# Top-k attention with a squared-ReLU MLP on one core: top-k on folded halves, a mask applied in PSUM, and a planned order

## The chip, the cores and the metric

One core of a Trainium2 chip runs the whole program. The metric is the device time of one execution in microseconds (us). Three runs of the kernel before gave 2025.48, 2029.64 and 2031.14 us; their median is 2029.64 us. The engines are named as in the profile: PE is the matrix engine (PEld its weight loads), DVE the vector engine, ACT the scalar engine, POOL the GpSimd engine, SP the engine that issues the DMAs.

## The reference

```python
def _attn_ref(q, k, v):                       # each (8, 8, 576, 64) float32
    scores = scale * np.matmul(q, k.transpose(0, 1, 3, 2))     # scale = 1/8
    kth = np.partition(scores, -32, axis=-1)[..., -32:-31]
    scores = np.where(scores >= kth, scores, -1000000000.0)
    attn = np.exp(scores - np.max(scores, axis=-1, keepdims=True))
    attn = attn / (np.sum(attn, axis=-1, keepdims=True) + 1e-09)
    return np.matmul(attn, v)

def _moe_ref(x, w_in, w_out):                 # x (4608, 512), w_in (512, 2048), w_out (2048, 512)
    r = np.maximum(x @ w_in, 0.0)
    return (r * r) @ w_out
```

The attention output of all heads is laid out as 4608 tokens by 512 and goes through the second function. So each of 8 x 8 x 576 = 36864 query rows has to find the 32nd largest of its 576 scores.

## The kernel before, in words

**Tiling.** Two heads make a pair, 32 pairs in all. The 1152 query rows of a pair are cut into 9 blocks of 128 rows (block 4 has 64 rows of either head), so there are 288 blocks. All of a block lives on 128 partitions, with its 576 scores along the free dimension.

**One block.** PE transposes q and k of the pair once (L238 to L265) and computes the scores in float32, with 64 rows of contraction (L316, L317). ACT copies them from PSUM to `Ssb` (L328). DVE finds the 32nd largest of 576 values in four rounds: MAX8 gives the eight largest, MATCH_REPLACE8 takes them out (L341 to L347; each MATCH_REPLACE8 brings a short MATCH_VALUE_LOAD), and a compare writes a bias `Bsb`, 0 or -30000 (L348). POOL adds bias and scores (L362). ACT takes the exponential with its row sum (L380), DVE the reciprocal (L390), ACT scales an identity matrix by it (L402), PE multiplies by that matrix, which transposes and normalises at once (L417, L418), ACT copies the result to bfloat16 `pT` (L430, L431). When the 9 blocks of a pair are there, PE computes the product with v, with 64 output rows per head (L461, L468), and ACT puts it into `xT`.

Every DVE and every ACT instruction waits for the one before it on its engine (`_run`, L117 to L128), since each round reads what the last one wrote.

**MLP.** Tokens go through it in 9 chunks of 512: 16 groups of 4 matmuls into one PSUM bank `Hps` (L546), ReLU and square on ACT (L563, L565), then 16 matmuls for each 128 tokens (L580) into the same bank, a copy (L600) and a DMA out.

**What sets the order.** Every step is a task with a hand-written time, counted in blocks (L434 to L443 for the attention, L492 to L498 for the product with v, L638 to L647 for the MLP); each engine runs its tasks sorted by that time and waits on semaphores. SP issues four weight loads first, each waiting for POOL's cast of the one before (L179 to L185), and only then the loads of q, k and v.

```python
            run_dve(lambda: vec.max(m8[:, 0, :], ssb[:, :]))
            run_dve(lambda: vec.match_replace(T1[:, :], m8[:, 0, :], ssb[:, :], NEG_MR))
            run_dve(lambda: vec.max(m8[:, 1, :], T1[:, :]))
```

Of the kernel before, what the change touches and what calls it, by code (L numbers as in the profile page):

```python
# [3 lines left out]
ALU = mybir.AluOpType  # L5
ACTF = mybir.ActivationFunctionType
FP32 = mybir.dt.float32
BF16 = mybir.dt.bfloat16

NEGB = -30000.0  # L10
NEG_MR = -3.0e38
TOPK = 32
P = 128


def bass_top_k_attn__then__act_relu_squared_kernel(
# [7 lines left out]
    n_batches_override=None,  # L24
):
    Bq, Hq, S, Dh = q.shape
    assert Hq == 8 and S == 576 and Dh == 64, (Bq, Hq, S, Dh)
    NB = Bq if n_batches_override is None else n_batches_override
# [15 lines left out]
    ident_bf = sb("ident_bf", [P, P], BF16)

    Rq = [sb(f"Rq{i}", [P, 5, 2, Dh]) for i in range(2)]
    Rk = [sb(f"Rk{i}", [P, 5, 2, Dh]) for i in range(2)]
    Rv = [sb(f"Rv{i}", [P, 5, 2, Dh]) for i in range(2)]
    qT = [sb(f"qT{i}", [P, S]) for i in range(2)]
    kT = [sb(f"kT{i}", [P, S]) for i in range(2)]  # L50
    vbf = [sb(f"vbf{i}", [P, 5, 2, Dh], BF16) for i in range(2)]

    KSB, KM, KE, KD, KZ = 5, 2, 3, 3, 4
    Ssb = [sb(f"Ssb{i}", [P, S]) for i in range(KSB)]
    T1 = sb("T1", [P, S])
    T2 = sb("T2", [P, S])
    Bsb = [sb(f"Bsb{i}", [P, S]) for i in range(2)]
    Smask = [sb(f"Smask{i}", [P, S]) for i in range(KM)]
    negm = [sb(f"negm{i}", [P, 1]) for i in range(KM)]
    M8 = [sb(f"M8_{i}", [P, 4, 8]) for i in range(2)]  # L60
    Ebf = [sb(f"E{i}", [P, S], BF16) for i in range(KE)]
    Zt = sb("Z", [P, KZ])
    rZt = sb("rZ", [P, KZ])
    Dt = [sb(f"Dt{i}", [P, P], BF16) for i in range(KD)]
    pT = [sb(f"pT{i}", [P, 5, 2 * S], BF16) for i in range(2)]
    xT = sb("xT", [P, NCT, NTOK], BF16)

# [48 lines left out]

    def _run(engkey, eng, op, inc):  # L117
        s, n = prog[engkey]
        if n > 0:
            eng.wait_ge(s, n)  # L120
        ins = op()
        if inc is None:
            ins.then_inc(s, 1)
        else:
            ins.then_inc(inc[0], inc[1])
            eng.nop().then_inc(s, 1)
        prog[engkey][1] = n + 1
        return ins  # L128

    def run_dve(op, inc=None):  # L130
        return _run("dve", nc.vector, op, inc)

    def run_act(op, inc=None):
        return _run("act", nc.scalar, op, inc)

    def block_parts(g):
        if g < 4:
            return [(0, 128 * g, 128, 0)]
        if g == 4:
            return [(0, 512, 64, 0), (1, 0, 64, 64)]  # L140
        qs = 128 * g - 576
        return [(1, qs, 128, 0)]

    def gp_setup():
        g = nc.gpsimd
        g.memset(ident32[:], 0.0).then_inc(s_set, 1)
        g.wait_ge(s_set, 1)
        g.affine_select(ident32[:], ident32[:], [[-1, P]], ALU.not_equal, 1.0,
                        base=0, channel_multiplier=1).then_inc(s_set, 1)
        g.wait_ge(s_set, 2)  # L150
        g.tensor_copy(ident_bf[:], ident32[:]).then_inc(s_set, 1)

    task("gp", -100, 0, gp_setup)

    WST4 = wst[:, :].rearrange("p (ct f) -> p ct f", ct=NCT)
    WST8 = wst[:, :].rearrange("p (fb o) -> p fb o", fb=8)

    def gp_weights():
        g = nc.gpsimd
        g.wait_ge(s_dw, 16 * 1)  # L160
        g.wait_ge(s_set, 3)
        g.tensor_copy(win[:, :, 0:1024], WST4).then_inc(s_wc, 1)
        g.wait_ge(s_dw, 16 * 2)
        g.wait_ge(s_wc, 1)
        g.tensor_copy(win[:, :, 1024:2048], WST4).then_inc(s_wc, 1)
        g.wait_ge(s_dw, 16 * 3)
        g.wait_ge(s_wc, 2)
        g.tensor_copy(wo[:, 0:8, :], WST8).then_inc(s_wc, 1)
        g.wait_ge(s_dw, 16 * 4)
        g.wait_ge(s_wc, 3)  # L170
        g.tensor_copy(wo[:, 8:16, :], WST8).then_inc(s_wc, 1)

    task("gp", -50, 0, gp_weights)

    def sp_weights():
        spe = nc.sync
        wi = moe_w_in.rearrange("(ct p) f -> p ct f", p=P)
        wo_ap = moe_w_out.rearrange("(fb p) o -> p fb o", p=P)
        spe.dma_start(WST4, wi[:, :, 0:1024]).then_inc(s_dw, 16)  # L179
        spe.wait_ge(s_wc, 1)  # L180
        spe.dma_start(WST4, wi[:, :, 1024:2048]).then_inc(s_dw, 16)
        spe.wait_ge(s_wc, 2)
        spe.dma_start(WST8, wo_ap[:, 0:8, :]).then_inc(s_dw, 16)
        spe.wait_ge(s_wc, 3)
        spe.dma_start(WST8, wo_ap[:, 8:16, :]).then_inc(s_dw, 16)  # L185

    task("sp", -90, 0, sp_weights)

    def dq_val(pi):
        return 128 * (pi // 2 + 1)  # L190

    def dv_val(pi):
        return 64 * (pi // 2 + 1)

    def sp_pair_dma(pi):
        def fn():
            spe = nc.sync
            b, hp = pi // NHP, pi % NHP
            slot = pi % 2
            if pi >= 2:  # L200
                spe.wait_ge(s_qkt, 4 * (pi - 1))
                spe.wait_ge(s_cv, pi - 1)
                spe.wait_ge(s_dq[slot], dq_val(pi - 2))
                spe.wait_ge(s_dvr[slot], dv_val(pi - 2))
            for (src, R, semx) in ((q, Rq[slot], s_dq[slot]),
                                   (k, Rk[slot], s_dq[slot]),
                                   (v, Rv[slot], s_dvr[slot])):
                for h in range(2):
                    sh = src[b, 2 * hp + h, :, :]
                    spe.dma_start(  # L210
                        R[:, 0:4, h, :],
                        sh[0:512, :].rearrange("(tb p) d -> p tb d", p=P),
                    ).then_inc(semx, 16)
                    spe.dma_start(
                        R[0:64, 4, h, :],
                        sh[512:576, :],
                    ).then_inc(semx, 16)
        return fn

    for pi in range(NPAIR):  # L220
        task("sp", 9 * pi - 18, 0, sp_pair_dma(pi))

    def pe_qk_transpose_round(pi, r):
        def fn():
            pe = nc.tensor
            slot = pi % 2
            base = 4 * pi
            if r == 0:
                pe.wait_ge(s_set, 2)
                pe.wait_ge(s_dq[slot], dq_val(pi))  # L230
                for (sx, vx) in ops_waits[("tq", pi)]:
                    pe.wait_ge(sx, vx)
            else:
                pe.wait_ge(s_qke, base + r)
            mm = None
            if r == 0:
                for tb in range(4):
                    mm = pe.matmul(  # L238
# [473 lines left out]
```

## Time and profile before

| | |
|---|---|
| median of three runs | 2029.64 us (2025.48 to 2031.14) |
| profiled execution, first to last instruction | 2029.7 us |
| DVE busy | 1730.8 us, 85% |
| PE busy | 1383.1 us, 68% |
| ACT busy | 1076.7 us, 53% |
| POOL busy | 419.6 us, 21% |
| granted PE clock, mean | 0.667 of full speed |

The profile's page gives only the span of the profiled execution, and that equals the median of the runs, so nothing measurable lies around it. A busy PE is not a PE at its peak, since its matmuls overlap; the granted clock has two levels, 0.5 (1.2 GHz) and 1.0 (2.4 GHz), and a value between them is a mean over a stretch.

### The profile page before, as it was taken

Reading aid. Unit: us, or ns where it says so; the run is one execution under the profiler, and the core shown is the slowest. Engines: PE = TensorE matmul, PEld = TensorE weight load, DVE = VectorE, ACT = ScalarE, POOL = GpSimd, SP = SyncE. Lnnn points to the kernel's source line nnn. Section 1 sums busy time; section 2 is a strip of 40 time slices with the busy share of each in tenths; the row PEclk is TensorE's granted clock in tenths of the full one; section 3 lists DMA queues with packets and bytes.
Section 4 is the critical chain, followed back from the end, with each engine's and each line's share of the span. In section 5 each row is a group of like instructions: output and inputs, shape, how many; then the busy total and the mean of one; then the engine's idle time right before and its main releaser. Section 6 shows DMA issues by size and latency. Waiting matters only on the chain.

```text
span 2029.7 us, 23123 instructions
## 1 busy us (share of the span) xinstructions
PE 1383.1 (68%) x4764; PEld 632.4 (31%) x4832; DVE 1730.8 (85%) x3456; ACT 1076.7 (53%) x2597; POOL 419.6 (21%) x299
## 2 busy tenths in 40 slices
PE   0556567777667776877667767777678776778576
PEld 0223333333333332333333333333333333333222
DVE  0899999998999999998999989999999989998500
ACT  0354555664566554664566555664566645664434
POOL 3122222222222222221222222221222222222100
PEclk9995555776566755677567765677555865666569
DMA  5100000001000100001000110001000100000000
GB/s 188 30 18 18 18 18 18 18 9 31 18 18 18 34 23 18 1 23 34 18 18 18 29 28 1 18 19 39 18 18 18 28 12 18 18 1 21 0 16 26
DMA packets 125197, 47.65 MB, mean 23 GB/s; under 512 B 117376, under 2 KB 117376, under 8 KB 125056
## 3 DMA queue, kind: packets, MB, share of 16 engines
q1 hardware_dynamic: 125056, 46.16, 8.6%
q8 instruction: 40, 0.66, 0.1%
q14 instruction: 101, 0.83, 0.1%
HBM read 36.70 MB, written 9.44 MB: 23 GB/s over the span
## 4 chain that ended last, share of the span: by engine, by line
DVE 55%; PE 20%; issue 12%; ACT 8%; DMA 1%; DVEq 1%; POOL 1%; ACTq 0%; SPq 0%; POOLq 0%
DVE T L342 8%; DVE T L346 8%; DVE T L344 8%; DVE M L345 8%; DVE M L347 8%; DVE M L343 8%; PE Hps L546 7%; DVE M L341 7%; PE Hps L580 5%; PE Ops L461 3%; ACT gT L563 2%; PE Tst L417 2%; DVE rZ L390 1%; ACT pT L430 1%; PE Ops L253 1%
## 5 line engine op out<-in xcount | busy, mean ns | idle before, releaser
L362 POOL TENSOR_TENSOR Smask<-Ssb,Bsb 128x576 f32<-128x576 f32 x288 | 404.2, 1403 | 1453.1 <-DVE Bsb L348 1448.0
L316 PE MATMUL Sps<-kT,qT 64*128 64x512 f32 (+1 forms) x640 | 499.2, 957 | 0.3 <-ACT kT L283 0.3
L417 PE MATMUL Tst<-Dt,E 128*128 128x128 bf16 x1152 | 151.7, 276 | 447.3 <-ACT pT L431 443.4
L341 DVE MAX8 M<-Ssb 128x8 f32<-128x576 f32 x288 | 214.5, 745 | 104.6 <-ACT Ssb L328 55.4
L402 ACT ACTIVATE Dt<-ident_bf,rZ 128x128 bf16<-128x128 bf16 x288 | 116.1, 403 | 306.0 <-DVE rZ L390 305.2
L546 PE MATMUL Hps<-xT,win 128*128 128x512 bf16 x531 | 221.8, 552 | 29.9 <-ACT gT L563 20.7
L417 PEld LDWEIGHTS Tst<-Dt,E 128*128 128x128 bf16 x1152 | 90.2, 117 | 486.1 <-ACT E L380 468.1
L317 PEld LDWEIGHTS Sps<-kT,qT 64*128 64x128 f32 (+1 forms) x640 | 156.3, 262 | 247.9 <-issue 247.9
L380 ACT ACTIVATE E<-Smask,negm 128x576 bf16<-128x576 f32 x288 | 223.1, 775 | 9.4
L345 DVE MAX8 M<-T 128x8 f32<-128x576 f32 x288 | 219.1, 761 | 9.8
L347 DVE MAX8 M<-T 128x8 f32<-128x576 f32 x288 | 219.1, 761 | 9.8
L343 DVE MAX8 M<-T 128x8 f32<-128x576 f32 x288 | 219.0, 760 | 9.8
L342 DVE MATCH_REPLACE8 T<-M,Ssb 128x576 f32<-128x576 f32 x288 | 213.8, 742 | 0.0
L346 DVE MATCH_REPLACE8 T<-M,T 128x576 f32<-128x576 f32 x288 | 213.8, 742 | 0.0
L344 DVE MATCH_REPLACE8 T<-M,T 128x576 f32<-128x576 f32 x288 | 213.7, 742 | 0.0
L328 ACT COPY Ssb<-Sps 128x576 f32<-128x576 f32 x288 | 184.2, 639 | 9.5 <-PE Sps L317 7.0
L580 PE MATMUL Hps<-wo,gT 128*128 128x512 bf16 x553 | 169.3, 455 | 11.8 <-ACT osb L600 4.6
L563 ACT ACTIVATE gT<-Hps 128x512 bf16<-128x512 f32 x144 | 85.7, 595 | 156.8 <-PE Hps L546 120.0
L430 ACT CAST pT<-Tst 128x512 bf16<-128x512 f32 x288 | 162.7, 565 | 2.3 <-PE T L418 2.3
L348 DVE TENSOR_SCALAR Bsb<-Ssb,M 128x576 f32<-128x576 f32 x288 | 149.8, 520 | 10.3
L316 PEld LDWEIGHTS Sps<-kT,qT 64*128 64x128 f32 (+1 forms) x640 | 120.4, 254 | 110.8 <-issue 102.5
L461 PE MATMUL Ops<-pT,vbf 128*64 128x512 bf16 (+1 forms) x320 | 135.8, 559 | 4.7 <-issue 3.3
(45 smaller groups left out, 1156.0 us busy)
## 6 DMA issues: line engine op xcount, KB each, us to landing
out_dram<-osb SPq DMA_DIRECT2D x36, 256.0 KB, 2.0
Rq<-in_q_dram SPq DMA_DIRECT2D x64, 128.0 KB, 2.3
Rk<-in_k_dram SPq DMA_DIRECT2D x64, 128.0 KB, 2.4
Rv<-in_v_dram SPq DMA_DIRECT2D x64, 128.0 KB, 2.4
wst<-in_moe_w_in_dram SPq DMA_DIRECT2D x2, 2048.0 KB, 7.9
wst<-in_moe_w_out_dram SPq DMA_DIRECT2D x2, 2048.0 KB, 8.9
Rq<-in_q_dram SPq DMA_DIRECT2D x64, 16.0 KB, 2.1
Rk<-in_k_dram SPq DMA_DIRECT2D x64, 16.0 KB, 2.1
```

The source lines that it names most:

```text
L316: last = pe.matmul(sps[rb:rb + nr, 0:512], qTi, kTi[:, 0:512])
L341: run_dve(lambda: vec.max(m8[:, 0, :], ssb[:, :]))
L342: run_dve(lambda: vec.match_replace(T1[:, :], m8[:, 0, :], ssb[:, :], NEG_MR))
L343: run_dve(lambda: vec.max(m8[:, 1, :], T1[:, :]))
L344: run_dve(lambda: vec.match_replace(T2[:, :], m8[:, 1, :], T1[:, :], NEG_MR))
L345: run_dve(lambda: vec.max(m8[:, 2, :], T2[:, :]))
L346: run_dve(lambda: vec.match_replace(T1[:, :], m8[:, 2, :], T2[:, :], NEG_MR))
L347: run_dve(lambda: vec.max(m8[:, 3, :], T1[:, :]))
L362: g.tensor_tensor(sm[:, :], ssb[:, :], bsb[:, :], ALU.add).then_inc(s_gm, 1)
L417: last = pe.matmul(Tst[:, j, :], e[:, 128 * j:128 * j + 128], d[:, :])
L546: last = pe.matmul(Hps[:, 0:ln], win[:, ct, fb * 128:fb * 128 + 128], xT[:, ct, ts:ts + ln], start=(ct == 0), stop=(ct == NCT - 1),)
L580: last = pe.matmul(Hps[0:nr, 0:DMODEL], gT[:, fb, o:o + nr], wo[:, fb, :], start=(fb == 0), stop=(fb == NFB - 1),)
```

## The change

The kernel is written anew around the same data types. For each query block:

- The 576 scores are kept as two halves of 288. DVE takes the larger of each column pair (`m`). POOL gets the smaller of each pair exactly, by adding the two bit patterns as integers (`t1`) and subtracting that of the larger (`lo`). DVE runs the four MAX8 and three MATCH_REPLACE8 on the 288 larger values and one MAX8 on the 288 smaller ones. The 32nd largest of all is then the largest of: the 32nd of the larger ones, and for j = 1 to 8 the smaller of the j-th of the smaller ones and the (32-j)-th of the larger ones (`mn`, `kt`). It holds if fewer than 8 of the smaller ones are among the 32 largest; a flag at the end says whether a row broke that, and if so the whole program is run a second time with 16 smaller ones.
- POOL makes a mask tile `w` in bfloat16 with two instructions of 576 columns: it is 2 to the 60th where a score falls short, and else the row's largest score, but not under zero.
- PE computes the scores a second time, transposed (keys on partitions), and subtracts the mask in the same PSUM bank by a matmul with the negative identity. ACT takes the exponential straight into the layout that the product with v needs.
- The product with v is token-major: 65 columns per head and block, the last one of ones, so that the row sum comes with it. DVE takes its reciprocal and multiplies; PE transposes the result back.
- Blocks go in groups of 2, 2, 2 and 3 (one block of either head side by side), and the DVE instructions of a group alternate between its blocks. The two heads' float32 matmuls are issued alternately, one on partitions 0 to 63 and one on 64 to 127, into different banks.
- The MLP runs per batch (576 tokens) with two PSUM banks per group; of the last batch the square is on DVE. Weights come in 16 loads of 512 KB, behind the first loads of q and k.
- A planner (`Plan.schedule`) runs all steps through an event loop with an estimated duration each, on every engine the ready step with the lowest priority value first, and hands out the buffers. The engines get the resulting fixed orders; `Emitter` puts waits only where a step needs something not yet known to be done, on its own engine too.

```diff
-            run_dve(lambda: vec.max(m8[:, 0, :], ssb[:, :]))
...
-            run_dve(lambda: vec.tensor_scalar(bsb[:, :], ssb[:, :], m8[:, 3, 7:8], NEGB,
-                                              ALU.is_lt, ALU.mult), inc=(s_tk, 1))
...
-            g.tensor_tensor(sm[:, :], ssb[:, :], bsb[:, :], ALU.add).then_inc(s_gm, 1)
...
+    GROUPS = [[(0, 0), (1, 0)], [(0, 1), (1, 1)], [(0, 2), (1, 2)], [(0, 3), (1, 3), (2, 4)]]
+    PER = 3.6
...
+                            for half in range(2):
+                                ks = HALF * half
+                                for h in range(2):
+                                    ins = mm(bank(tiles[h], half)[:, 0:HALF],
+                                             x[64 * h:64 * h + 64, 0, 128 * gi:128 * gi + 128],
+                                             x[64 * h:64 * h + 64, 1, ks:ks + HALF], True)
...
+                    for i in range(nb):
+                        pl.op("gp", .85, tg - 1 + .8 * i, lambda t=t1[i], s=st[i]: gp.tensor_tensor(
+                            at(t)[:, :].bitcast(I32), at(s)[:, 0:HALF].bitcast(I32),
+                            at(s)[:, HALF:S].bitcast(I32), ALU.add), r=[st[i]], w=[t1[i]], take=[t1[i]])
+                        dve(.38, lambda t=m[i], s=st[i]: vec.tensor_tensor(
+                            at(t)[:, :], at(s)[:, 0:HALF], at(s)[:, HALF:S], ALU.max),
...
+                        pl.op("gp", .85, tg + .8 + .8 * i, lambda t=t1[i], m_=m[i], l=lo[i]: gp.tensor_tensor(
+                            at(l)[:, :].bitcast(I32), at(t)[:, :].bitcast(I32),
+                            at(m_)[:, :].bitcast(I32), ALU.subtract), r=[t1[i], m[i]], w=[lo[i]], take=[lo[i]])
+                    for rnd in range(4):
+                        for i in range(nb):
+                            src = m[i] if rnd == 0 else wk[i]
+                            last[i] = dve(.38, lambda s=src, i=i, rnd=rnd, A=A: vec.max(
+                                A(i, 8 * rnd, 8 * rnd + 8), at(s)[:, :]), r=[src], w=[a])
...
+                            f = (lambda s=src, d=wk[i], i=i, rnd=rnd, A=A: vec.match_replace(
+                                at(d)[:, :], A(i, 8 * rnd, 8 * rnd + 8), at(s)[:, :], NEG))
...
+                        bl[i] = dve(.38, lambda l=lo[i], i=i, B=B: vec.max(B(i, 0), at(l)[:, :]),
...
+                    mn = dve(.1, lambda a=a, bt=bt, nb=nb, n0=n0, nr=nr: vec.tensor_tensor(
...
+                    sh = dve(.08, lambda a=a, nb=nb, n0=n0: vec.tensor_scalar(
...
+                    kt = dve(.1, lambda a=a, nb=nb, n0=n0, nr=nr: vec.tensor_reduce(
...
+                        pl.op("gp", .65, tw + 1.3 * i, lambda y=y, s=st[i], n=n0 + i: gp.tensor_scalar(
+                            at(y)[:, :], at(s)[:, :], nkth[:, n:n + 1], STEEP, ALU.add, ALU.mult),
...
+                        pl.op("gp", .65, tw + 1.3 * i + .65, lambda y=y, w=w, n=n0 + i: gp.tensor_scalar(
+                            at(w)[:, :], at(y)[:, :], BIG, shift[:, n:n + 1], ALU.min, ALU.max),
...
+                        for j in range(2):
+                            ins = mm(o[:, 128 * j:128 * j + 128], at(ws[(h, j)])[:, kc:kc + nk],
+                                     neg_bf[:, :], False)
...
+                                for h in range(2):
+                                    qkT(bank(e, h)[:, 0:nq], qk, h, 128 * kb, 128, q0, nq, True)
+                                for h in range(2):
+                                    ins = masked(bank(e, h)[:, 0:nq], h, 128 * kb, 128, ws, wz)
...
+                                mm(o[:, 65 * u:65 * u + 65], pp[:, kb, h, 128 * j:128 * j + 128],
+                                   vv[:, 4 * h + kb, :], first_)
...
+                    pl.op("dve", .15, tt + 9, lambda av=av, rz=rz, nu=nu: vec.reciprocal(
...
+                    pl.op("dve", .45, tt + 9.1, lambda av=av, rz=rz, xr=xr, nu=nu: vec.tensor_tensor(
...
+            val = eng.value_load(flag[0:1, 0:1], min_val=0, max_val=P)
+            with eng.If(val > 0):
+                em.emit(again, e, eng)
```

## Rows read from the trace of the kernel before

**Rows 1.** The page's first part: busy time and share of the span by engine.
```profile
PE 1383.1 (68%) x4764; PEld 632.4 (31%) x4832; DVE 1730.8 (85%) x3456; ACT 1076.7 (53%) x2597; POOL 419.6 (21%) x299
```
**Rows 2.** Waits: engine, line, whom it waited for: us in total, times, longest.
```profile
DVE M L341 <- ACT Ssb L328: 55.4, 1, 55.4
...
PE Ops L238 <- DMA Rk<-in_k_dram: 47.4, 1, 47.4
...
DVE M L341 <- issue: 44.5, 28, 3.5
```
**Rows 3.** Timeline of DVE, one block in mid-run: start us, us, line, operation.
```profile
1007.11 0.52 DVE L348 TENSOR_SCALAR Bsb<-Ssb,M 128x576 f32<-128x576 f32 x1
1007.55 0.16 DVE L390 RECIPROCAL rZ<-Z 128x1 f32<-128x1 f32 x1
1007.62 0.74 DVE L341 MAX8 M<-Ssb 128x8 f32<-128x576 f32 x1
1008.40 0.09 DVE L342 MATCH_VALUE_LOAD T<-M,Ssb 128x8 f32 x1
1008.48 0.74 DVE L342 MATCH_REPLACE8 T<-M,Ssb 128x576 f32<-128x576 f32 x1
...
1013.35 0.52 DVE L348 TENSOR_SCALAR Bsb<-Ssb,M 128x576 f32<-128x576 f32 x1
```
**Rows 4.** Busy time by engine over the top-k stage.
```profile
55.00:1905.00 1850.00, 1292.76 (x4465) 601.40 (x4525) 1730.62 (x3455) 1023.46 (x2505) 402.92 (x288) 0.65 0.08 19
```
**Rows 5.** Groups of POOL by shape: busy us, mean ns; then one instruction in its timeline.
```profile
L362 POOL TENSOR_TENSOR Smask<-Ssb,Bsb 128x576 f32<-128x576 f32 x288 | 404.2, 1403 | 1453.1 <-DVE Bsb L348 1448.0 <-ACT Ssb L328 5.1
L162 POOL CAST win<-wst 128x4096 bf16<-128x4096 f32 x1 | 3.6, 3602 | 6.9 <-DMA wst<-in_moe_w_in_dram 6.9
L151 POOL CAST ident_bf<-ident 128x128 bf16<-128x128 f32 x1 | 0.3, 291 | 0.1
...
1007.71 1.41 POOL L362 TENSOR_TENSOR Smask<-Ssb,Bsb 128x576 f32<-128x576 f32 x1 [4.84 <-DVE Bsb L348]
```
**Rows 6.** Timeline of PE at clock 1.0: a whole block, small matmuls, block 4.
```profile
144.82 1.12 PE L316 MATMUL Sps<-kT,qT 64*128 64x512 f32 x2
145.79 0.33 PE L317 MATMUL Sps<-kT,qT 64*128 64x64 f32 x2
147.43 0.38 PE L417 MATMUL Tst<-Dt,E 128*128 128x128 bf16 x4 [1.31 <-ACT pT L431]
147.74 0.24 PE L418 MATMUL T<-Dt,E 128*64 128x128 bf16 x1
...
452.22 0.60 PE L238 MATMUL Ops<-ident,Rq 128*128 128x128 f32 x4
...
472.15 1.08 PE L316 MATMUL Sps<-kT,qT 64*64 64x512 f32 x4
473.06 0.29 PE L317 MATMUL Sps<-kT,qT 64*64 64x64 f32 x4
```
**Rows 7.** Timeline of PE in the MLP at the end, at 1.0.
```profile
1981.47 1.02 PE L546 MATMUL Hps<-xT,win 128*128 128x512 bf16 x4 [0.72 <-issue]
...
2014.13 3.61 PE L580 MATMUL Hps<-wo,gT 128*128 128x512 bf16 x16 [0.77 <-ACT osb L600]
```
**Rows 8.** Two-microsecond stretches of the MLP at the end; granted clock third from the end.
```profile
1964.00:1966.00 2.00, 2.00 (x6) 0.72 (x5) 0.00 (x0) 0.00 (x0) 0.00 (x0) 0.50 0.00 0
1966.00:1968.00 2.00, 1.60 (x7) 0.48 (x5) 0.00 (x0) 0.36 (x1) 0.00 (x0) 0.90 0.00 0
...
1988.00:1990.00 2.00, 1.04 (x4) 0.31 (x4) 0.00 (x0) 1.50 (x3) 0.00 (x0) 1.00 0.00 0
```
**Rows 9.** SP's timeline at the start: one of a pair's 12 issues.
```profile
45.33 0.59 SPq L210 DMA_DIRECT2D Rv<-in_v_dram  x1
```
**Rows 10.** ACT's exponential and copy by shape: busy us, mean ns.
```profile
L380 ACT ACTIVATE E<-Smask,negm 128x576 bf16<-128x576 f32 x288 | 223.1, 775 | 9.4
L328 ACT COPY Ssb<-Sps 128x576 f32<-128x576 f32 x288 | 184.2, 639 | 9.5 <-PE Sps L317 7.0 <-issue 1.9 <-DVE Bsb L348 0.2
```

More of the change, by code (lines that the diff above doesn't have):

```diff
@@ L2 @@
+import heapq
 import concourse.bass as bass
@@ L6, with __init__, take, find @@
 ACTF = mybir.ActivationFunctionType
+AX = mybir.AxisListType
 FP32 = mybir.dt.float32
 BF16 = mybir.dt.bfloat16
-NEGB = -30000.0
-NEG_MR = -3.0e38
+I32 = mybir.dt.int32
+P = 128
 TOPK = 32
-P = 128
+NEG = -3.0e38
+BIG = 2.0 ** 60
+STEEP = -(2.0 ** 90)
+class Pool:
+    def __init__(self, name, n):
+        self.name, self.n = name, n
+        self.free = list(range(n))
+        self.last = [None] * n
+        self.made = self.taken = 0
+    def take(self, tl):
+        if self.name != "psum" and tl.num != self.taken:
+            return None
+        s = self.find(tl.width)
+        if s is not None:
+            self.taken += 1
+        return s
+    def find(self, width):
+        if width == 1:
+            if not self.free:
+                return None
+            if self.name == "psum":
+                half = [s for s in self.free if (s ^ 1) not in self.free]
+                s = half[0] if half else self.free[0]
+            else:
+                s = self.free[0]
+            self.free.remove(s)
+            return s
+        for s in self.free:
+            if s % width == 0 and all(s + i in self.free for i in range(width)):
+                for i in range(width):
+                    self.free.remove(s + i)
+                return s
+        return None
+    def undo(self, s, width):
+        self.taken -= 1
+        self.give(s, width)
+    def give(self, s, width):
+        self.free.extend(range(s, s + width))
@@ new lines, with __init__ @@
+class Tile:
+    def __init__(self, pool, width=1):
+        self.pool, self.width = pool, width
+        self.slot = None
+        self.num = pool.made
+        pool.made += 1
+        self.ops = []
+        self.writers = []
+        self.left = 0
+        self.prev = []
+        self.taker = None
+class Op:
+    __slots__ = ("eng", "dur", "prio", "fn", "deps", "tiles", "takes", "n", "users", "start", "end",
+                 "idx", "sem", "val", "ndma", "seq", "vc", "waits", "wars", "later")
@@ L23, in bass_top_k_attn__then__act_relu_squared_kernel @@
     out: bass.AP,
[L24 removed]
 ):
[L26 to L28 removed]
+    NB, H, S, D = q.shape
+    assert H == 8 and S == 576 and D == 64, (NB, H, S, D)
+    HALF = S // 2
     NHP = 4
@@ L649, in bass_top_k_attn__then__act_relu_squared_kernel @@
-    n_tot = NMOUT
-    n_even = (n_tot + 1) // 2
-    n_odd = n_tot // 2
-    def sp_final():
-        spe = nc.sync
-        spe.wait_ge(s_dout[0], 16 * n_even)
-        spe.wait_ge(s_dout[1], 16 * n_odd)
-    task("sp", chunk_t0(NCHUNK - 1) + 200, 0, sp_final)
-    with nc.Block() as blk:
-        def emit(eng):
-            for _, _, _, fn in sorted(tasks[eng], key=lambda x: (x[0], x[1], x[2])):
-                fn()
+        for i in range(16):
+            s = tile("ws")
+            if i < 8:
+                ct, half = divmod(i, 2)
+                src = wi[:, ct, 1024 * half:1024 * half + 1024]
+                dst = win[:, ct, 1024 * half:1024 * half + 1024]
+                view = lambda s: at(s)[:, :]
+            else:
+                fb = 2 * (i - 8)
+                src = wo_ap[:, fb:fb + 2, :]
+                dst = wo[:, fb:fb + 2, :]
+                view = lambda s: at(s)[:, :].rearrange("p (f o) -> p f o", f=2)
+            pl.op("sp", 4.0, 20 + 4 * i, lambda s=s, src=src, view=view: [nc.sync.dma_start(view(s), src)],
+                  w=[s], take=[s], ndma=1, sem=lambda o: f"ws{o.takes[0].slot}")
+            weights.append(pl.op("gp", 1.1, 40 + 6 * i, lambda s=s, dst=dst, view=view: gp.tensor_copy(dst, view(s)),
+                                 r=[s]))
@@ new lines, in setup, with fin @@
+        setup.pre = [i1, i2, i3] + ones + [f1]
+        return weights
+    main = build(False, True, setup)
+    for o in main.ops:
+        if o not in setup.pre and o.eng == "pe":
+            o.deps.update(setup.pre)
+    def fin(pl, waits):
+        vec, pe = nc.vector, nc.tensor
+        t = Tile(psum)
+        c = pl.op("dve", .35, 1e6, lambda: vec.tensor_tensor(
+            fcmp[:, :], b8all[:, :, 7], nkth[:, :], ALU.add), after=waits)
+        d = pl.op("dve", .35, 1e6, lambda: vec.tensor_reduce(fone[:, 0:1], fcmp[:, :], AX.X, ALU.max), after=[c])
+        f = pl.op("dve", .1, 1e6, lambda: vec.tensor_scalar(
+            fone[:, 0:1], fone[:, 0:1], 0.0, None, ALU.is_gt), after=[d])
+        g = pl.op("pe", .1, 1e6, lambda: pe.matmul(bank(t)[0:1, 0:1], fone[:, 0:1], fone[:, 1:2],
+                                                   start=True, stop=True), w=[t], take=[t], after=[f])
+        return pl.op("dve", .1, 1e6, lambda: vec.tensor_copy(flag[:, :], bank(t)[0:1, 0:1]), r=[t])
@@ new lines, in bass_top_k_attn__then__act_relu_squared_kernel @@
+    flagged = fin(main, list(kths))
+    span = main.schedule()
+    em.number(main)
+    again = build(True, False, None)
+    t_end = max(o.end for o in main.ops) + 1
+    again.schedule(t_end)
+    em.number(again)
+    out_waits = [(em.dma[k][0], 0, k) for k in em.dma if k.startswith("o")]
+    first_tot = {}
+    for pl_, store in ((main, first_tot),):
+        for o in pl_.order["sp"]:
+            if o.idx[0][1].startswith("o"):
+                store[o.idx[0]] = o.idx[1]
+    second_tot = {}
@@ new lines, in bass_top_k_attn__then__act_relu_squared_kernel, with emit @@
+    for o in again.order["sp"]:
+        if o.idx[0][1].startswith("o"):
+            second_tot[o.idx[0]] = o.idx[1]
+    with nc.Block() as blk:
+        def emit(e, eng):
+            em.emit(main, e, eng)
+            if e == "sp":
+                for kk, vv in first_tot.items():
+                    eng.wait_ge(em.sem(kk), vv)
+            if e != "dve" or True:
+                eng.wait_ge(em.sems["dve"], flagged.idx[1])
+            val = eng.value_load(flag[0:1, 0:1], min_val=0, max_val=P)
+            with eng.If(val > 0):
+                em.emit(again, e, eng)
+                if e == "sp":
+                    for kk, vv in second_tot.items():
+                        eng.wait_ge(em.sem(kk), vv)
```

1113 lines of the change are left out of this document (552 added, 561 removed).

## The prediction

> **What bounds the kernel now.** I read the engine shares first [rows 1]: DVE is busy for 85% of the span, nobody else for more than 68%. The waits say whether it rests inside its stage [rows 2]: it waits once for 55.4 us, for the first scores, and after that 44.5 us in 28 places, all of them with no releaser. The stage view gives 1850 us from first to last DVE work, 1730.62 of them busy [rows 4]. The timeline of one block shows why [rows 3]: from one TENSOR_SCALAR to the next are 6.24 us, and 288 x 6.24 = 1797 us; the stage is 1850 / 1797 = 1.029 of that. Then comes a tail without DVE, 2029.7 - 1905 = 125 us, in which the MLP catches up. So the time is 55 (start) + 1850 (top-k on DVE) + 125 (MLP): those three terms are what the change must move. The span equals the median of the runs, so I sum against 2029.7.
>
> **DVE, the new top-k.** One price per column: MAX8 over 576 columns takes 0.74 us and a one-column RECIPROCAL 0.16 [rows 3], so a column costs (0.74 - 0.16) / 575 = 1.0 ns and an instruction over 288 columns 0.16 + 0.29 = 0.45 us; the same for MATCH_REPLACE8, which took 0.74 too. How far apart do they start? An instruction that depends on its forerunner comes 0.04 us after its end (MAX8 lasts 0.74, the next starts 0.78 after it). One that does not starts early: RECIPROCAL begins 0.44 us after a TENSOR_SCALAR of 0.52, and MAX8 0.07 us after RECIPROCAL [rows 3]. The new order alternates between the blocks of a group, so most forerunners belong to another block: 0.45 - 0.08 = 0.37 us per instruction, and 0.08 more for each MATCH_VALUE_LOAD. Per block:
> - five MAX8 (four on the larger values, one on the smaller): 5 x 0.37 = 1.85
> - three MATCH_REPLACE8 with their loads: 3 x 0.45 = 1.35
> - one maximum of the halves, a two-input operation that before never ran on DVE: between 0.37 (as MAX8) and 0.49 (it waits for ACT's copy just ahead); I take 0.49.
>
> That is 3.69 us, times 288 = 1063 us. Small instructions per pair: three for each of four groups (`mn`, `sh`, `kt`), between 0.07 and 0.20 us by the RECIPROCAL row, and as they follow one another in part I take 0.13, 12 x 0.13 = 1.56; and twice a reciprocal (0.20) with a multiply of up to 320 columns (0.16 + 0.32 + 0.04 = 0.52), 1.44. Together 3.0 x 32 = 96 us. The sum 1159 us times the 1.029 that this stage loses today gives 1193 us, 37.3 us per pair. With every doubt settled low it is 1028 + 57 = 1085; with every instruction held until its forerunner ends it is 9 x 0.49 plus 3 x 0.08 = 4.65 per block, (1339 + 123) x 1.029 = 1504.
>
> **POOL** gets most of the new work. Its old 128x576 add took 1.403 us; casts of 4096 and 128 columns took 3.602 and 0.291, so 0.83 ns a column over 0.18 us [rows 5]. Integer add and subtract over 288 columns: 0.18 + (1.403 - 0.18) / 2 = 0.79 each. Mask in two one-input instructions of 576 columns: 0.18 + 0.48 = 0.66 each, if they run like a cast; like the two-input add, 1.40. With 0.1 us between instructions (an estimate from the spacing of the chain's dependent steps on DVE, 0.04, and doubled for POOL) a block costs 2 x 0.79 + 2 x 0.66 + 0.4 = 3.3 us; the casts of v add 1.1 per pair: 30.8 us per pair, under DVE's 37.3. MAX8 at 1007.62 and MATCH_REPLACE8 at 1008.48 ran beside POOL's add of 1007.71 [rows 3, 5] and took no longer than elsewhere, so I charge nothing for running side by side.
>
> **PE.** Column counts per pair: 20 score matmuls of 288 columns are ten blocks of 576, and the transposed scores as many again. A whole block at full clock is 0.97 + 0.33 = 1.30 us; block 4, which holds 64 rows of each head on separate array rows, does both heads' 576 columns in 0.91 + 0.29 = 1.20 us [rows 6]. Two heads side by side thus cost one; the new order issues all of them so, ten pairs x 1.20 = 12.0 us. Fifty mask matmuls, fifty with v and six transposes at (147.74 - 147.43) / 4 = 0.078: 8.3. Transposes of q and k: 1.4. MLP per batch: 16 x 1.02 x 1.125 (2304 columns for 2048) + 5 x 3.61 = 36.4 [rows 7], a quarter of it 9.1. Sum 30.8 us per pair at clock 1.0, under DVE's 37.3; at the 0.65 that the stage has now [rows 4] it would be 47.4, over it. I take the high clock: in the MLP a solid run of matmuls lifted it from 0.50 to 1.00 and PE then kept it at half its time busy [rows 8], and here it has 30.8 / 37.3 = 83% to do.
>
> **ACT and SP.** Nine copies of 0.64, exponentials over 5184 columns at no more than nine of 0.78 [rows 10], q, k and result copies 2.0, MLP 37 x 0.64 / 4 = 5.9: 20.7 us per pair, hidden. Twelve loads per pair at 0.59 us of SP's time [rows 9] are 7 of 37 us, hidden; stores and later loads stand behind loads that wait for a free buffer, with 30 us to spare.
>
> **Start and end.** DVE starts at 55.4 now because q and k landed at 47.4, behind three casts of weights [rows 2]. With q and k first: 8 loads x 0.59, 2 us to land (47.4 less 45.3, when the first load behind k was issued [rows 9]), and of the 8.0 us that followed to DVE about 5, with three banks instead of one: 12 us. At the end, after the last top-k: six mask instructions 4.0, transposed scores and masks of the last half 5.7, exponential 0.6, product with v 2.3, DVE 0.7, transpose and copy 1.1; then the last batch's MLP 36.4, its groups back to back in two banks where now 0.7 us of waiting stands before each [rows 7], and 4 for its first fill, last copy and store (an estimate): 55 us. The flag and the branch are in no row: 0 to 3 us, beside the stores; I take 0.
>
> Sum: 12 + 1193 + 55 = **1260 us**.
>
> **New waits.** DVE's reciprocal now waits for the product with v, and the next group's MAX8 stand behind it in DVE's fixed order; PE's masks wait for POOL, and the next scores and the MLP stand behind them. Whatever runs behind the plan on PE or POOL thus stops DVE.
>
> **Rivals.**
> - *DVE and POOL block each other.* No row shows a two-input DVE instruction beside POOL. If it has to wait for the POOL instruction in progress, half of 0.72 us at 30.8 / 37.3 = 83% of all times, it loses 0.30; 288 maxima and 128 `mn` make 125 us: 1385 us. The Trainium skill, SBUF — State Buffer, Who interferes with whom, states just that: a VectorE instruction with two SBUF inputs contends with a GpSimd one that reads SBUF, and the later one blocks entirely. For: POOL is nearly always reading. Against: MAX8, with one input, shows nothing. Chance 0.24.
> - *POOL is the bound*, its mask instructions at 1.40: 4.8 us per block, 44.1 per pair, 32 x 44.1 + 67 = 1478. Chance 0.06.
> - *PE is the bound*: the two heads run one after the other (26.0 instead of 12.0, 44.8 per pair, 1501 us), or side by side at clock 0.65 (47.4, 1584 us). Block 4 speaks against the first; the present mean clock, with PE 70% busy in the stage, for the second. Chance 0.11.
> - *Slower than before*: both at once. Matmuls with 64 rows of contraction are two thirds of PE's work then, the stage with such matmuls has clock 0.65 today, and 44.8 / 0.65 = 68.9 us per pair gives 2272. It decides from (2029.7 - 67) / 32 = 61.3 us per pair on. Chance 0.04.
> - *The second pass runs.* Counted on the reference's inputs, at most 6 column pairs of a row lie both among its 32 largest (in 3 of 36864 rows), and 8 are needed. It would about double the time. Chance 0.01.
>
> **How the numbers follow.** The forecast keeps 0.54. Its low end is 12 + 1085 + 55 = 1152, with no loss at all, which I round to 1160; the high end takes in the mutual blocking with some loss (1385) and reaches to POOL's bound, 1470. About 0.05 lies below and 0.15 above. A measurement of this kernel tells about 0.3% from no change (its three runs span 0.28%); faster 0.95, the same 0.00, slower 0.05.
>
> **What would show it.** Right: MAX8 of 288 columns lasts 0.45 us and starts 0.37 after its forerunner; DVE over 90% busy from 12 us to 55 before the end; granted clock over 0.85; one-input POOL instructions near 0.66. Wrong: two-input maxima far over 0.45, or gaps before them that end with POOL (the blocking); DVE idle before the reciprocal, released by PE (PE the bound); PE's pairs of float32 matmuls starting a full matmul apart; POOL over 95% busy.

## The result, and the profile of the changed kernel

The changed kernel takes 1232.33 us (median of four runs, 1230.77 to 1232.97); the kernel before took 2030.39 us in the runs beside it (2025.48 to 2032.98). The ratio is 0.6069, with a 95% interval of 0.606 to 0.6079. The forecast of 1260 us is 2.2% too high and its range holds the result. The profiled execution took 1230.77 us with a span of 1229.0 us.

First the page of the changed kernel: engine shares, and the chain that ended last by engine. They answer to [rows 1].

```profile
PE 956.7 (78%) x7938; PEld 570.8 (46%) x7938; DVE 1154.5 (94%) x3988; ACT 576.3 (47%) x953; POOL 986.4 (80%) x1282
...
DVE 89%; PE 4%; POOL 3%; SPq 1%; issue 1%; DMA 1%; ACT 0%; POOLq 0%
```

DVE is still the bound, now with little rest. Next its waits, and the longest one of PE, which cost nothing as long as DVE had work:

```profile
PE ps L352 <- POOL w L561: 167.0, 60, 9.0
...
DVE m L510 <- ACT s L482: 18.4, 1, 18.4
...
DVE rz L672 <- PE ps L352: 15.2, 3, 13.6
...
DVE b8all L533 <- POOL lo L513: 4.5, 3, 2.7
```

The 18.4 us are the start; 13.6 of the 15.2 are one wait after the last top-k, outside the stage. In the stage, from 18.4 us to the last `kt` at 1169.6, DVE waits for hardly anything. A view over most of that stage (busy time of PE, PEld, DVE, ACT, POOL, then the granted clock, DMA share and GB/s) answers to [rows 4]:

```profile
150.00:1050.00 900.00, 733.77 (x6253) 438.70 (x6252) 900.00 (x3139) 455.99 (x758) 767.01 (x989) 0.91 0.14 34
```

PE is busy for 82% of it at a granted clock of 0.91, where the stage of before had 0.65. The groups by line and shape tell what DVE and POOL spend (busy us, mean ns of one):

```profile
L519 DVE MAX8 a<-wk 128x8 f32<-128x288 f32 x864 | 351.4, 451 | 0.0
L525 DVE MATCH_REPLACE8 wk<-a,wk 128x288 f32<-128x288 f32 x576 | 251.5, 449 | 0.0
L513 POOL TENSOR_TENSOR lo<-t,m 128x288 int32<-128x288 int32 x288 | 249.4, 883 | 88.1 <-DVE m L510 58.8 <-DVE a L543 29.3
L507 POOL TENSOR_TENSOR t<-s 128x288 int32<-128x288 int32 x288 | 228.6, 808 | 15.1
L561 POOL TENSOR_SCALAR w<-y,shift 128x576 bf16<-128x576 f32 x288 | 214.1, 743 | 29.8
...
L510 DVE TENSOR_TENSOR m<-s 128x288 f32<-128x288 f32 x288 | 148.2, 517 | 18.4 <-ACT s L482 18.4
...
L547 DVE TENSOR_SCALAR shift<-a 128x2 f32<-128x2 f32 x96 | 55.2, 575 | 0.0
...
L440 POOL TENSOR_SCALAR vb<-rv,heads 128x64 bf16<-128x64 f32 x64 | 47.2, 745 | 0.0
L543 DVE TENSOR_TENSOR a<-b8all,a 128x16 f32<-128x16 f32 x96 | 35.2, 367 | 0.0
```

MAX8 and MATCH_REPLACE8 of 288 columns last the forecast 0.45 us. Two groups look wrong for their size: `shift` computes two numbers per row and takes 0.575 us on average, `mn` (L543) computes 16 and takes 0.367, while the RECIPROCAL of [rows 3] took 0.16. The timeline of DVE at the border of two groups, and of POOL in the same time, suggests why:

```profile
606.21 0.79 DVE L510 TENSOR_TENSOR m<-s 128x288 f32<-128x288 f32 x1
606.92 0.76 DVE L543 TENSOR_TENSOR a<-b8all,a 128x16 f32<-128x16 f32 x1
607.61 0.45 DVE L510 TENSOR_TENSOR m<-s 128x288 f32<-128x288 f32 x1
607.98 0.76 DVE L547 TENSOR_SCALAR shift<-a 128x2 f32<-128x2 f32 x1
```

```profile
605.95 0.74 POOL L561 TENSOR_SCALAR w<-y,shift 128x576 bf16<-128x576 f32 x1
606.77 0.88 POOL L507 TENSOR_TENSOR t<-s 128x288 int32<-128x288 int32 x1
607.61 1.84 POOL L513 TENSOR_TENSOR lo<-t,m 128x288 int32<-128x288 int32 x2
```

`m` starts while POOL is in `w`, and lasts 0.79 us; `mn` starts while POOL is in `t`, and ends 0.03 us after it; `shift` starts while POOL is in the first `lo`, and lasts 0.76. The second `m` starts as `t` gives way to `lo`, and lasts 0.45. Sixteen microseconds later the small ones are short, though POOL is not idle:

```profile
623.10 0.45 DVE L510 TENSOR_TENSOR m<-s 128x288 f32<-128x288 f32 x1
623.46 0.17 DVE L543 TENSOR_TENSOR a<-b8all,a 128x16 f32<-128x16 f32 x1
...
623.91 0.17 DVE L547 TENSOR_SCALAR shift<-a 128x2 f32<-128x2 f32 x1
```

```profile
622.76 1.56 POOL L440 TENSOR_SCALAR vb<-rv,heads 128x64 bf16<-128x64 f32 x2
```

Here POOL is the one held up. The second of these two `vb` (v in bfloat16, 64 columns) starts at 623.18, after the first `m`, and lasts 1.14 us; the 64 instructions of this line have a median of 0.447 us, and the mean of 0.745 above hides that 31 of them last 0.50 to 1.57. `lo` too has a mean of 0.883 us over a median of 0.80. So it looks as if either engine can hold up the other.

So the theory after the result: DVE alone is the bound; the mutual blocking that the prediction had as a rival is there and costs DVE time, but other terms were charged too high by about as much. To be told apart: whether these long instructions are blocking at all, whether DVE's alternating order and PE's alternating heads are really what the forecast rests on, and where the start comes from.

### The profile page after: what moved, and what is told of

Same layout as the page of the kernel before. It is cut to its first block, busy times and chain, and to the rows that moved or that the text cites. A ratio compares the mean times of both kernels' runs of the same rounds, so it can differ in the third digit from the quotient of the medians.

```text
span 1229.0 us, 23132 instructions
## 1 busy us (share of the span) xinstructions
PE 956.7 (78%) x7938; PEld 570.8 (46%) x7938; DVE 1154.5 (94%) x3988; ACT 576.3 (47%) x953; POOL 986.4 (80%) x1282
## 4 chain that ended last, share of the span: by engine, by line
DVE 89%; PE 4%; POOL 3%; SPq 1%; issue 1%; DMA 1%; ACT 0%; POOLq 0%
DVE a L519 32%; DVE wk L525 29%; DVE m L510 9%; DVE b8all L533 8%; DVE shift L547 5%; PE ps L352 4%; DVE a L543 2%; DVE x L674 2%; DVE nkth L549 1%; POOL y L558 1%; POOL w L561 1%; POOL win L784 0%; POOL t L507 0%; POOL lo L513 0%; DVE rz L672 0%
## 5 line engine op out<-in xcount | busy, mean ns | idle before, releaser
L352 PE MATMUL ps<-qk 64*128 64x288 f32 (+5 forms) x2560 | 469.5, 478 | 203.0 <-POOL w L561 167.0
L352 PEld LDWEIGHTS ps<-qk 64*128 64x128 f32 (+1 forms) x2560 | 226.5, 195 | 325.6 <-POOL w L561 182.8
L519 DVE MAX8 a<-wk 128x8 f32<-128x288 f32 x864 | 351.4, 451 | 0.0
L513 POOL TENSOR_TENSOR lo<-t,m 128x288 int32<-128x288 int32 x288 | 249.4, 883 | 88.1 <-DVE m L510 58.8
L482 ACT COPY s<-ps 128x576 f32<-128x576 f32 x288 | 175.8, 641 | 245.6 <-POOL y L558 146.8
L525 DVE MATCH_REPLACE8 wk<-a,wk 128x288 f32<-128x288 f32 x576 | 251.5, 449 | 0.0
L558 POOL TENSOR_SCALAR y<-s,nkth 128x576 f32<-128x576 f32 x288 | 213.9, 743 | 33.6 <-DVE nkth L549 4.7
L507 POOL TENSOR_TENSOR t<-s 128x288 int32<-128x288 int32 x288 | 228.6, 808 | 15.1
L561 POOL TENSOR_SCALAR w<-y,shift 128x576 bf16<-128x576 f32 x288 | 214.1, 743 | 29.8
L510 DVE TENSOR_TENSOR m<-s 128x288 f32<-128x288 f32 x288 | 148.2, 517 | 18.4 <-ACT s L482 18.4
L352 PE MATMUL ps<-wo,g 128*128 128x512 bf16 (+1 forms) x640 | 158.1, 385 | 0.0
```

The source lines that it names most:

```text
L352: return pe.matmul(o, l, r, start=start, stop=stop, skip_group_check=True)
L482: pl.op("act", .67, tg - 6 + i, lambda s=st[i], p_=sp[i]: act.copy(at(s)[:, :].rearrange("p (a c) -> p a c", a=2), ps32[:, p_.slot:p_.slot ...
L507: pl.op("gp", .85, tg - 1 + .8 * i, lambda t=t1[i], s=st[i]: gp.tensor_tensor(at(t)[:, :].bitcast(I32), at(s)[:, 0:HALF].bitcast(I32), at( ...
L510: dve(.38, lambda t=m[i], s=st[i]: vec.tensor_tensor(at(t)[:, :], at(s)[:, 0:HALF], at(s)[:, HALF:S], ALU.max), r=[st[i]], w=[m[i]], take= ...
L513: pl.op("gp", .85, tg + .8 + .8 * i, lambda t=t1[i], m_=m[i], l=lo[i]: gp.tensor_tensor(at(l)[:, :].bitcast(I32), at(t)[:, :].bitcast(I32) ...
L519: last[i] = dve(.38, lambda s=src, i=i, rnd=rnd, A=A: vec.max(A(i, 8 * rnd, 8 * rnd + 8), at(s)[:, :]), r=[src], w=[a])
```

## The experiments

Times are to be compared with 1232.33 us. The experiments are variants of the changed kernel, and their diffs are shortened to the calls that change. Experiments 2, 3 (with its control) and 4 are one execution each, the others four.

**1. `shift` by an operation with one input and no scalar.** The tile `a` gets a 49th column that stays 0.

```diff
-  vec.tensor_scalar(shift[:, n0:n0 + nb], at(a)[:, 0:nb, 0], 0.0, None, ALU.max)
+  vec.tensor_reduce(shift[:, n0:n0 + nb], at(a)[:, 0:nb, 0:49:48], AX.X, ALU.max)
```

> Theory (blocking): the shift instruction of each group, a TENSOR_SCALAR on 2 or 3 columns, mean 0.575 us in the changed kernel's trace, lasts that long because it needs the SBUF port that POOL holds; a TENSOR_REDUCE on the same tile, nkth, lasts 0.16. Written as a TENSOR_REDUCE against a zero column, shift should last about 0.17 and start its successor 0.08 later instead of 0.52: 128 x 0.44 = 57 us less, about 1175 us. Rival (own cost): a small strided instruction in that place takes 0.5 us whatever its kind: about 1232 us, shift still near 0.5. Second rival (the wait moves on): the next two-input maxima wait in its place: 1200 to 1225 us.

1198.91 us (1198.04 to 1200.01), 33 us less. The groups of `shift` and `m` here:

```profile
L547 DVE TENSOR_REDUCE shift<-a 128x2 f32<-128x4 f32 x96 | 14.0, 146 | 0.0
...
L510 DVE TENSOR_TENSOR m<-s 128x288 f32<-128x288 f32 x288 | 158.8, 552 | 18.6 <-ACT s L482 18.6
```

TENSOR_REDUCE is not held up: 0.146 us, with more columns to read. The time lies just under the range of the second rival, for only 33 of the 58 us that `shift` no longer takes from start to start are gained: `m` grew from 0.517 to 0.552 us and `mn` from 0.367 to 0.380 (15 and 3 us from start to start), and DVE waits 7.0 us for `lo` instead of 4.5. The instruction that used to wait out POOL's `lo` is gone, and others now meet POOL.

**2. POOL's add and subtract cut to 32 columns.** It leaves out 256 of the 288 minima of a row; `lo` is filled with -9 at the start.

```diff
-  at(l)[:, :].bitcast(I32), at(t)[:, :].bitcast(I32), at(m_)[:, :].bitcast(I32), ALU.subtract)
+  at(l)[:, 0:32].bitcast(I32), at(t)[:, 0:32].bitcast(I32), at(m_)[:, 0:32].bitcast(I32), ALU.subtract)
```

> Leaves out 256 of 288 columns of POOL's integer add and subtract, so the smaller values are mostly missing; DVE's instructions are unchanged. Theory (blocking): shift and mn wait for the add or subtract that POOL starts as soon as the maxima are there; with those at about 0.25 us instead of 0.81 and 0.88, shift falls from a mean of 0.575 to below 0.35 and mn from 0.367 to below 0.25, and the time by 30 to 60 us, to 1170 to 1200 us. Rival (own cost): shift stays near 0.575, the time at 1225 to 1235 us, since POOL was not the bound.

1148.78 us, 84 less, and 21 below the range of the theory. DVE's instructions are the same and in the same order; the groups that were long are short, and so is POOL's `vb`, which was not touched:

```profile
L519 DVE MAX8 a<-wk 128x8 f32<-128x288 f32 x864 | 347.9, 443 | 0.0
...
L510 DVE TENSOR_TENSOR m<-s 128x288 f32<-128x288 f32 x288 | 129.2, 449 | 18.7 <-ACT s L482 18.7
...
L547 DVE TENSOR_SCALAR shift<-a 128x2 f32<-128x2 f32 x96 | 21.7, 226 | 0.0
L543 DVE TENSOR_TENSOR a<-b8all,a 128x16 f32<-128x16 f32 x96 | 16.6, 173 | 0.0
```

```profile
L440 POOL TENSOR_SCALAR vb<-rv,heads 128x64 bf16<-128x64 f32 x64 | 27.8, 442 | 0.0
```

From one start to the next (added up over DVE's timeline from 150 to 1050 us) `m` fell from 0.411 to 0.362 us, `shift` from 0.523 to 0.144 and `mn` from 0.220 to 0.088. That is 288 x 0.049 + 128 x 0.379 + 128 x 0.132 = 80 us, nearly all of the gain; MAX8 moved from 0.362 to 0.364, so it was not held up. This is the price of the blocking.

**3. No alternation.** The seven MAX8 and MATCH_REPLACE8 of a block are issued before those of the next, and the planner's gap of 0.07 us between dependent instructions of one engine is set to 0 so that it keeps this order.

```diff
-  for rnd in range(4):
-      for i in range(nb):
+  for i in range(nb):
+      for rnd in range(4):
```

> The seven MAX8 and MATCH_REPLACE8 of a block are issued block after block, no longer alternating. Theory (an instruction that depends on its forerunner starts 0.04 us after its end, another one 0.08 before): MAX8 starts 0.48 us after its forerunner instead of 0.36; seven links of a block x 0.12 us x 288 = 242 us more, about 1470 us. Rival (instructions are spaced by their length alone): no change, 1225 to 1245 us.

1420.76 us. The timeline of DVE in the first round, in the changed kernel and here:

```profile
609.51 0.44 DVE L525 MATCH_REPLACE8 wk<-a,m 128x288 f32<-128x288 f32 x1
609.87 0.08 DVE L525 MATCH_VALUE_LOAD wk<-a,m 128x8 f32 x1
```

```profile
608.57 0.44 DVE L523 MATCH_REPLACE8 wk<-a,m 128x288 f32<-128x288 f32 x1
609.04 0.46 DVE L519 MAX8 a<-wk 128x8 f32<-128x288 f32 x1
609.54 0.09 DVE L523 MATCH_VALUE_LOAD wk<-a,wk 128x8 f32 x1
```

Each now starts 0.03 us or more after the end of its forerunner, where it started 0.08 before. From start to start are 0.461 us for MAX8 of the larger values and 0.469 for MATCH_REPLACE8, where the changed kernel has 0.362 and 0.359, with durations as before. Less than the 1470 expected, in part because `shift` (0.173 us) hardly meets POOL in this order. As two things were changed, a control followed that sets only the planner's gap to 0:

> A control for the third experiment: only the planner's constant of 0.07 us between dependent instructions of one engine is set to 0, and the 7 instructions of a block still alternate between the blocks of a group. If the alternation is what counted there: 1220 to 1250 us, MAX8 and MATCH_REPLACE8 still 0.36 us apart from start to start. If the constant counted, since the planner then no longer sees that an instruction behind its own forerunner starts later: MAX8 0.45 us apart in many places and over 1350 us.

1261.15 us, 11 above the first expectation; MAX8 of the larger values stays 0.376 us apart, so it is the first theory that holds. The gap alone costs 29 us, the alternation is worth 1420.76 - 1261.15 = 160 us. Where the 29 come from was followed no further; POOL waits 97.5 us for `nkth` instead of 4.7, and `m` takes 0.565.

**4. The two heads' float32 matmuls not alternated.**

```diff
-  for kk in range(2):
-      for h in range(2):
+  for h in range(2):
+      for kk in range(2):
```

(and likewise for the first scores and in the other loops over `h` of the transposed ones)

> The float32 matmuls of the two heads are no longer alternated: both of one head, then both of the other. Theory (heads alternated run side by side, and PE has slack at that price): PE's float32 work goes from 12 us per pair towards 26, its total from about 31 to as much as 45 us per pair against 36 on DVE, so PE becomes the bound: 1400 to 1520 us, DVE idle before its reciprocal or its first maximum. Rival (side by side only where both the rows and the columns of the array differ, or hidden slack large enough): 1225 to 1270 us.

1398.34 us, just under the expected range. PE becomes the bound; engine shares, and DVE's wait:

```profile
PE 1244.0 (89%) x7938; PEld 701.5 (50%) x7938; DVE 1172.1 (84%) x3988; ACT 579.4 (41%) x953; POOL 977.5 (70%) x1282
...
DVE rz L669 <- PE ps L352: 163.7, 39, 23.4
```

The granted clock from 150 to 1050 us is 0.88 where it was 0.91, too little to be the cause. The group shows which matmuls: the transposed ones with 320 columns, busy for 125.2 us in the changed kernel and 260.1 here.

```profile
L352 PE MATMUL ps<-qk 64*128 64x320 f32 x512 | 125.2, 571 | 123.0 <-POOL w L561 123.0
```

```profile
L352 PE MATMUL ps<-qk 64*128 64x320 f32 x512 | 260.1, 595 | 85.4 <-POOL w L561 85.4
```

So two heads side by side do cost one. The first scores of 288 columns hardly changed (168.4 to 180.6 us): two of one head and two of the other, with nothing between them, still run side by side; the transposed ones have the mask matmuls between the heads.

**5. The planner's estimate of a DMA issue.** It took 0.06 us for what lasts 0.59 on SP [rows 9].

```diff
-  hold = o.dur if e != "sp" else 0.06 * max(1, o.ndma)
+  hold = o.dur if e != "sp" else 0.57 * max(1, o.ndma)
```

> The planner is told that SP needs 0.57 us to issue a DMA, where it had 0.06; nothing else is changed. In the changed kernel PE transposes q of pairs 0 and 1 first and waits until 12.06 us for the second, so DVE starts at 18.4 us instead of the 12 that were forecast. Theory (the planner's wrong issue time put the second q ahead of the first k): k of pair 0 comes first, DVE starts at 12 to 13 us, the time falls by 5 to 6 us to about 1227. Rival (DVE then waits later for what was put back): 1230 to 1235 us.

1226.08 us (1225.57 to 1228.48), 6 less. In the changed kernel PE stood before a transpose of the second pair's q, though the first pair's k was what DVE needed:

```profile
4.72 1.09 PE L355 MATMUL ps<-ident,rq 128*128 128x128 f32 x4 [4.72 <-DMA rq<-in_q_dram]
12.06 1.11 PE L355 MATMUL ps<-ident,rq 128*128 128x128 f32 x4 [6.26 <-DMA rq<-in_q_dram]
12.97 1.06 PE L355 MATMUL ps<-ident,rk 128*128 128x128 f32 x4
```

With the planner told the true time, the first pair's k comes second:

```profile
6.93 1.12 PE L355 MATMUL ps<-ident,rk 128*128 128x128 f32 x4 [1.09 <-DMA rk<-in_k_dram]
```

DVE starts at 11.9 us instead of 18.4. The gain is those 6.5 us, but not they alone: in the profiled executions the stage is 3.5 us longer (1154.7 for 1151.2) and the end 1.8 shorter.

**6. Without the second pass**: no flag, no branch, no second program (it doesn't run on these inputs).

```diff
-  flagged = fin(main, list(kths))
-  again = build(True, False, None)
```

> Leaves out the flag, the branch and the code of the second pass (the output is the same on these inputs). Theory: they lie beside the last block and the stores and cost 0 to 3 us: 1229 to 1233 us. Rival (half the program's size matters for code loading): 1215 to 1225 us.

1236.89 us (1236.51 to 1236.97): 4.6 us slower with less to do, which neither theory expected. Two parts move against each other.

The stage, from the first maximum to the last `kt`, takes 1161.5 us where the changed kernel has 1151.2. DVE, up to the flag, and POOL run the same instructions in the same order, but on DVE some last longer: `shift` of two columns takes 0.626 us instead of 0.575 and `mn` 0.393 instead of 0.367, while `m` takes 0.489 instead of 0.517. How DVE and POOL fall in with each other has changed; why it did, the run doesn't show.

The end is 4.2 us shorter, and most of that is the price of the flag. From the last matmul to the end of the span (1235.2) are 3.4 us here:

```profile
1214.45 17.33 PE L352 MATMUL ps<-wo,g 128*128 128x512 bf16 x78
```

In the changed kernel they are 6.8 us, and in all nine runs with the flag 6.6 to 7.1. So reading the flag and branching stand behind the last store, not beside it, and cost 3.4 us there: in the trace of the changed kernel SP's wait for the stores ends at 1225.19 us, and its load of the flag starts at 1225.24.

**7. Edits 1 and 5 together.**

> The TENSOR_REDUCE form of shift (1198.91 us alone) together with the planner's issue time of 0.57 us. Theory: the two gains are in different places, the start and the middle, and add up: 1198.9 less 5 to 6, 1193 us. Rival (part of the gain is lost to a new wait): 1196 to 1202 us.

1184.73 us (1182.5 to 1185.3), the best version; ratio to the kernel before 0.5838 (0.5822 to 0.5853).

```profile
PE 939.5 (80%) x7894; PEld 560.4 (47%) x7938; DVE 1115.8 (95%) x3988; ACT 575.6 (49%) x953; POOL 977.5 (83%) x1285
...
L510 DVE TENSOR_TENSOR m<-s 128x288 f32<-128x288 f32 x288 | 159.2, 553 | 12.4 <-ACT s L482 12.4
```

It gains 14 us on experiment 1, not the 6 of an earlier start alone, so neither expectation holds: DVE's wait for `lo` (7.0 us) is gone and that for the product with v is down from 22.1 to 17.8. `m` (0.553 us) is now what meets POOL most.

**8. The maxima of a group issued together and early**, on top of 7, so that they would run while POOL has other work.

```diff
-  dve(.38, lambda t=m[i], s=st[i]: vec.tensor_tensor(
+  pl.op("dve", .38, tg - 2.2 + .4 * i, lambda t=m[i], s=st[i]: vec.tensor_tensor(
...
```

> As the run with both, and the maxima of a group are put about 2.2 us earlier in DVE's order, between the last rounds of the group before, so that POOL's subtract, which they release, no longer runs beside mn. Theory (blocking is set by what POOL does in that moment): mn falls from a mean of 0.38 us towards 0.2, the maxima keep what they lose by chance; 10 to 20 us less than the run with both, 1173 to 1185 us. Rival (POOL reads nearly always, so another instruction is met instead): within 5 us of the run with both.

1207.48 us (1205.38 to 1208.72), 23 slower than 7; both expectations missed. `m` takes 0.619 us, and its spacing rose from 0.458 to 0.526: 288 x 0.068 = 20 us. POOL is busy for 81% of the span, most of it with instructions of 0.75 to 0.86 us, and an early place met it more often: from 150 to 1050 us, 32 of 229 maxima start while POOL is idle, in experiment 7 it was 55 of 234.

A version in which POOL needs nothing from `m` was not tried.

## Why the prediction was right

The three terms, against 12 + 1193 + 55:

- **Blocks: 288 x 3.69 = 1063 forecast, 288 x 3.484 = 1003 measured.** The price per column was right (0.45 us). The spacing came out at 0.362 for 0.37; a MATCH_REPLACE8 with its load took 0.359 + 0.063 = 0.42 for 0.45; `m` took 0.41 for 0.49. Experiment 3 shows that the spacing hangs on the alternation: without it the step "0.45 - 0.08" fails by 0.1 us an instruction, as the high bound of the prediction had it.
- **Small instructions: 96 forecast, 134 measured.** This step failed. "I take 0.13" read `shift` and `mn` as one-column instructions next to the RECIPROCAL row, and `shift` takes 0.523 from start to start, `mn` 0.220; `kt` at 0.083 was as read. The reciprocals and the multiplies behind them took 29 us where 46 were charged.
- **"I charge nothing for running side by side"** failed with it: 80 us. The rows behind it were of MAX8 and MATCH_REPLACE8, which indeed aren't held up; experiments 1 and 2 show that instructions with two inputs and the small TENSOR_SCALAR are. One of the prediction's own signs of being wrong was there: 49 of the 288 maxima last over 0.6 us, the longest 1.33. The rival named the mechanism and priced it at 125 us, on the wrong instructions: it put 0.30 on each of 288 maxima, which lose 0.05 (of 227 between 150 and 1050 us, 99 start while POOL is idle and 75 beside `vb`, which lasts 0.50 us or more in 50 of these and so is mostly the one to wait), and on each `mn`, which loses 0.13, and left out `shift`, which loses 0.38. The Trainium skill, SBUF — State Buffer, Who interferes with whom, was cited for the two-input case alone; it also lists `tensor_scalar` among the operations that can take the port shared with GpSimd, on conditions for its operands, and `tensor_reduce` as one that on trn2 never contends. The runs agree with both, 0.575 and 0.146 us for the same result. That the prediction did not look `shift` up there is its plainest omission.
- **The factor 1.029**, 34 us, was charged too high: the stage is 1151 us, 1.012 of the 1138 that the measured spacings add up to.
- **Start: 12 forecast, 18.4 measured**; the 12 were there to be had, as experiment 5 shows with 11.9. What failed is the assumption that PE takes the first pair's k right behind its q.
- **End: 55 forecast, 59 measured** (1169.6 to 1229.0). The MLP took 34.9 us for the 36.4 forecast, and three parts took longer. POOL's six mask instructions ended 5.7 us after the last `kt`, for 4.0. From there to the MLP are 11.9 us, for 10.4: PE had been busy for 0.19 us of those 5.7, and the first three of four tiles of transposed scores ran at a granted clock of 0.50, with 1.44 us where the fourth, after the clock had risen, took 0.81. And from the last matmul on are 6.8 us, for 4, of which the flag is 3.4 (experiment 6); "beside the stores; I take 0" failed:

```profile
1175.31 1.44 PE L352 MATMUL ps<-qk 64*128 64x320 f32 x4 [3.90 <-POOL w L561]
...
1181.29 0.81 PE L352 MATMUL ps<-qk 64*128 64x320 f32 x4
...
1187.23 17.52 PE L352 MATMUL ps<-xt,win 128*128 128x288 bf16 x128 [0.74 <-ACT xt L696]
1204.59 17.55 PE L352 MATMUL ps<-wo,g 128*128 128x512 bf16 x80
```

Together: +6 at the start, -60 in the blocks, +38 in the small ones, -20 of loss, +4 at the end, so 1260 - 32 = 1228 against a span of 1229.0. That the total was right to 2% is in part luck, since errors cancelled: 0.49 for `m`, taken for a wait on ACT that isn't there, loads and multiplies charged without overlap, and the factor 1.029 paid for the blocking that wasn't charged.

That the other engines stay hidden behind DVE held as argued. POOL was busy for 986.4 us, 30.8 per pair; the forecast's 30.8 had 3.6 of gaps in it, so POOL's work was dearer than forecast, by the mask (0.743 for 0.66), `lo` (0.883 for 0.79) and `vb`. PE kept the high clock (0.91 in the stage), which bears out the choice of "over 0.85"; ACT took 18 us per pair for 20.7. Of the rivals, POOL and PE as bounds did not come, and experiment 4 shows how near PE is: 287 us of busy time more and it sets the end at 1398, below the rival's 1501, in part because the first scores stayed side by side. (In the rival of a slower kernel, 26.0 of 44.8 us are 58%, not two thirds; nothing hangs on it.) The second pass did not run.

## What to carry to other kernels

Before two engines are planned side by side, look up every DVE instruction in the trace with POOL busy beside it, the smallest too: a TENSOR_SCALAR of two or three columns lost more here (49 us in 128 places) than the two-input maximum of 288 columns (14 us in 288), and the same number from a TENSOR_REDUCE lost nothing. Taking such a meeting away gives back only part of its price, since others move into its place, so measure the whole kernel. Where two variants differ by a few microseconds, read the stage and the end apart: in experiment 6 one grew by 10 us and the other shrank by 4. A long mean beside a busy neighbour need not be an instruction's own price: look at the shortest ones too, as `vb` shows. On DVE, alternating between independent chains was worth 160 us of 1421; telling the planner the true time of a DMA issue gave 6.

## What the runs showed of the hardware that was not expected

- A TENSOR_SCALAR on DVE with two results per row takes from 0.17 us (623.91) to 0.76 (607.98), by what POOL does; TENSOR_REDUCE, MAX8 and MATCH_REPLACE8 kept their durations in the changed kernel and all nine experiments (MAX8 of `wk` 0.440 to 0.460 us).
- POOL seems to be held up by DVE as well, though no experiment was made on that alone: its TENSOR_SCALAR of 64 columns (`vb`) takes 0.44 us on average in experiment 2, and from 0.43 to 1.57, 0.745 on average, in the changed kernel. The one of 576 columns (`w`) takes 0.743.
- The stage of an identical order of instructions on DVE and on POOL can differ by 10 us in 1151 (experiment 6).
